# One two-bank PSUM tile against two one-bank tiles in the experts' first layer

## The chip, the cores and the metric

The kernel runs on one core of a Trainium2 chip. What is measured is the device time of one execution in microseconds (us). Five engines matter: PE (TensorE: matmuls, and PEld, its weight loads), ACT (ScalarE), DVE (VectorE), POOL (GpSimd) and SP (SyncE, which issues the DMA transfers). Each runs its own list of instructions in order and waits on semaphores for the others. PE writes its results to PSUM, which has 8 banks of 512 float32 per partition; ACT and DVE read them from there.

## The reference

Three parts follow each other: attention with a computed position bias, a mixture of 8 dense experts, and one more feed-forward layer with an ELU.

```
scores = q @ kT / sqrt(D) + bias(log1p|i-j| / log1p(i))     # B=2, H=8, S=576, D=64
x = softmax(scores) @ v                                     # -> (1152, 512)
P = exp(x @ w_gate - max); 8 rounds of row and column normalising
out = sum over 8 experts e of P[:, e] * (relu(x @ w1[e]) @ w2[e])    # w1: 512x1024, w2: 1024x512
g = elu(out @ w_in)                                         # 512 x 2048
return g @ w_out                                            # (1152, 512)
```

## The kernel before, in words

The experts and the last layer run as one chain of 20 half layers `he` (two for each of the 8 experts, four for the last feed-forward layer; each takes 512 of the hidden columns), and each half layer in two token groups `n` of 2 x 256 and 2 x 320 tokens (`NN`). All products are made of a high and a low part (three matmuls instead of one).

**First layer.** A pair (half layer, token group) is worked in two units `u`. A unit is a 2 x 2 block product by Winograd's form of Strassen's method: seven products of six matmuls each (`product`, line 526, the matmul on L537), written to three PSUM banks b1, b2 and b3. The table `PROD` says which product goes to which bank, and `l1` (line 684) issues them in the order 1, (4 of the unit before), 2, 5, 6, 3, 7. Products 1, 6, 7 and 4 follow each other in b1, products 5 and 3 in b2, product 2 is in b3. After each product something empties or uses the bank (`evac`, line 651):

- `fork` (L550) on ACT copies a bank to SBUF: p1 and u2, u3 from b1, p5 from b2.
- `add` (L569) on DVE adds a bank and an SBUF tile: c1 from b3 and p1, then c1's second half from b2 and u2, and c22.
- `hidden` (L600, L603, and for the last layer L628 to L647) applies the activation and splits the result into hh and hl.

**Second layer.** `l2` (line 706, the matmul on L724) multiplies hh and hl with the second weights into a PSUM tile y. `step` (line 997) mixes the matmuls of one pair's second layer between the first-layer products of the next, so that some 3 to 5 y matmuls stand between two products. They are missing in three stretches: in the first pair (there is no second layer yet), around the change from the experts to the last layer, and partly in the last layer's first pairs.

**Where the order comes from.** `Plan` records every operation with its costs and dependences; `order` (line 137) sorts them, PE's main matmuls in a fixed order and the rest greedily by estimated times; `emit` then writes the program in that sorted order. Semaphores are not set by the plan: the tile framework sets them while the program is written, from what each instruction reads and writes, tile by tile, in the order in which they are written.

**PSUM before.** Pool psA has two buffers of two banks each, psB two banks, psC0 and psD one each: 8 banks in all. The attention uses psA for the score products (`emit_qk`, L1215, read on DVE by L1225), psB for transposes and y, psC0 and psD for the rest. `unit` (line 674) takes one psA buffer for a unit: b1 is its first bank and b2 its second, both in one tile named `m`. b3 is the one buffer of psC0.

Of the kernel before, what the change touches and what calls it, by code (L numbers as in the profile page):

```python
# [86 lines left out]
class Plan:  # L87
# [3 lines left out]
    def buf(self, tag, bufs, alloc, tile=None):  # L91
        b = Buf(tag, alloc, tile)
        q = self.tags.setdefault(tag, [])
        b.prev = q[-bufs] if len(q) >= bufs else None
        b.before = q[-1] if q else None
        if b.prev is not None:
            b.prev.closed = True
        b.closed = False
        q.append(b)
        return b  # L100
# [120 lines left out]
def attention_moe_elu_ffn_kernel(  # L221
# [16 lines left out]
    def sb(name, bufs, st=ctx, side="left"):  # L238
        return st.enter_context(tc.tile_pool(name=name, bufs=bufs, side=side, reuse_waits="tile"))
# [6 lines left out]
    stp = sb("st", 1)  # L246
    dr = ctx.enter_context(tc.tile_pool(name="dr", bufs=1, space=bass.MemoryType.DRAM))

    def psum(name, bufs, shape):
        p = ctx.enter_context(tc.tile_pool(name=name, bufs=bufs, space=bass.MemoryType.PSUM))  # L250
        return lambda nm: p.tile(shape, F32, tag=name, name=nm)

    psA = psum("psA", 2, [128, 2, 512])
    psB = psum("psB", 2, [128, 512])
    psC = [psum("psC", 1, [128, 512]), psum("psD", 1, [128, 512])]

    csb = cp.tile([128, C_TOT], F32, name="csb")
    ident = csb[:, C_ID:C_ID + 128]
# [12 lines left out]
    def do_bg(n):  # L271
        for _ in range(min(n, len(bg))):
            bg.pop(0)()
# [106 lines left out]
    def build():  # L380
        op, buf = plan.op, plan.buf
# [291 lines left out]

        def unit(he, n, u):
            N = NN[n]
            a = buf("psA", 2, lambda: psA("m"))
            b3 = buf("psC0", 1, lambda: psC[0]("m3"))
            x = {"key": (he, n, u), "b1": (a, 0), "b2": (a, 1), "b3": (b3, 0)}
            x["ap"] = lambda k: b3.get()[:, 0:N] if k == "b3" else a.get()[:, int(k[1]) - 1, 0:N]
            return x  # L680

        prev = [None]
# [1 line left out]
        def l1(he, n):  # L684
            for u in range(2):
                x = None
                for i in (1, 4, 2, 5, 6, 3, 7):
                    if i == 4:
                        if prev[0] is None:
                            continue  # L690
                        product(prev[0], 4)
                        evac(prev[0], 4)
                    else:
                        if x is None:
                            x = unit(he, n, u)
                        product(x, i)
                        evac(x, i)
                    yield i
                prev[0] = x
# [395 lines left out]
    def first_fill():  # L1095
        do_bg(999)
        pools["ops1"] = sb("ops1", 1)
        pools["h0"] = sb("h0", 4)
        pools["fk"] = sb("fk", 1)
        build()  # L1100
        for x in emit_it:
            if x == "attn":
                return
            yield
# [456 lines left out]
    with tc.manual_schedule():  # L1561
        moe(attention(first_fill))
# [58 lines left out]
```

## Time and profile before

| | us |
|---|---|
| median of 3 runs (1196.85 to 1201.21) | 1200.32 |
| the profiled execution: time of the run | 1198.01 |
| the profiled execution: span from the first to the last instruction | 1196.2 |
| PE busy in it | 1159.5 |
| DVE busy | 909.6 |
| ACT busy | 630.7 |
| mean granted TensorE clock, share of full speed | 0.997 |

The profile names an instruction by its line, engine, operation and tiles (`m<-oh,w1h`: writes m from oh and w1h). A row of the timeline gives the start, the duration, and in square brackets the idle time of the engine ahead of it with the instruction that ended it. Matmuls overlap each other in the timeline: the next starts while the one before still runs out, so the pace is the distance of the starts, not the duration.

The experts begin at about 203 us of the span, the last feed-forward layer's first products at about 980 us.

### The profile page before, as it was taken

What the parts mean: (1) busy time and instruction counts of PE and PEld (TensorE: products, weight loads), DVE (VectorE), ACT (ScalarE), POOL (GpSimd) and SP (SyncE); (2) the same over time, 40 slices, a digit from 0 to 9 for tenths busy, and PEclk for the clock granted to TensorE, in tenths of its full rate; (3) what the DMA queues carried; (4) which work ended last, traced back from release to release, by engine and by line L of the source; (5) the groups of instructions that cost most, each with busy time, mean ns of one, the idle gap of its engine ahead of it and who ended that gap; (6) DMA issues with size and microseconds to landing.
All of it is one profiled execution on the core that took longest, in us unless ns stands there. A gap on an engine that the chain in (4) does not pass through costs nothing.

```text
span 1196.2 us, 19633 instructions
## 1 busy us (share of the span) xinstructions
PE 1159.5 (97%) x7432; PEld 994.0 (83%) x7432; DVE 909.6 (76%) x1936; ACT 630.7 (53%) x1428; POOL 67.8 (6%) x91
## 2 busy tenths in 40 slices
PE   7899999999999999999999999999999988999998
PEld 3467988888888888888888888888888876788887
DVE  7887888745687777878778788787765468788875
ACT  7997677644244343444443434444434346677763
POOL 0103452000000000000000000000000002000000
PEclk9999999999999999999999999999999999999999
DMA  7876641111012223232333242333311101111102
GB/s 211 243 230 199 195 120 38 39 58 51 31 53 80 79 89 104 91 106 89 88 106 89 79 121 74 106 89 106 88 54 51 47 19 36 36 53 36 36 1 79
DMA packets 36286, 104.78 MB, mean 88 GB/s; under 512 B 4065, under 2 KB 4193, under 8 KB 36193
## 3 DMA queue, kind: packets, MB, share of 16 engines
q1 hardware_dynamic: 36192, 103.54, 28.3%
q8 instruction: 58, 0.95, 0.3%
q14 instruction: 36, 0.29, 0.1%
HBM read 81.88 MB, written 21.64 MB: 87 GB/s over the span
## 4 chain that ended last, share of the span: by engine, by line
PE 91%; ACT 2%; DVE 2%; issue 1%; POOL 0%; DVEq 0%; ACTq 0%; POOLq 0%
PE y L724 41%; PE m L537 38%; PE sc L1215 3%; PE av L1297 3%; PE tr L1266 2%; PE bps L1419 1%; PE av L1307 1%; PE av L1294 1%; PE lg L880 0%; ACT et L1240 0%; DVE ol L437 0%; PE trl L1278 0%; PE x2t L974 0%; DVE c L569 0%; ACT o L1451 0%
## 5 line engine op out<-in xcount | busy, mean ns | idle before, releaser
L537 PE MATMUL m<-oh,w1h 128*128 128x256 f32 (+1 forms) x1120 | 335.6, 300 | 3.8 <-DVE c L569 1.4
L537 PE MATMUL m<-oh,w1l 128*128 128x256 f32 (+1 forms) x1120 | 330.2, 295 | 3.8 <-ACT u L550 1.6
L537 PE MATMUL m<-ol,w1h 128*128 128x256 f32 (+1 forms) x1120 | 330.1, 295 | 2.8 <-DVE c L569 1.3
L724 PE MATMUL y<-w2h,hh 128*128 128x512 f32 x720 | 285.1, 396 | 2.8 <-ACT hh L644 1.5
L724 PE MATMUL y<-w2l,hh 128*128 128x512 f32 x720 | 283.2, 393 | 0.8 <-DVE w2l L437 0.8
L724 PE MATMUL y<-w2h,hl 128*128 128x512 f32 x720 | 283.4, 394 | 0.0
L537 PEld LDWEIGHTS m<-oh,w1h 128*128 128x128 f32 x1120 | 210.5, 188 | 46.3 <-ACT u L550 13.4
L537 PEld LDWEIGHTS m<-ol,w1h 128*128 128x128 f32 x1120 | 210.8, 188 | 22.8 <-DVE c L569 1.9
L537 PEld LDWEIGHTS m<-oh,w1l 128*128 128x128 f32 x1120 | 210.7, 188 | 5.6 <-ACT u L550 2.3
L724 PEld LDWEIGHTS y<-w2h,hh 128*128 128x128 f32 x720 | 135.3, 188 | 18.7 <-ACT hh L644 2.2
L724 PEld LDWEIGHTS y<-w2h,hl 128*128 128x128 f32 x720 | 135.1, 188 | 18.0
L550 ACT ACTIVATE p<-m 128x256 f32<-128x256 f32 (+1 forms) x160 | 65.7, 411 | 159.3 <-PE m L537 155.2
L724 PEld LDWEIGHTS y<-w2l,hh 128*128 128x128 f32 x720 | 135.3, 188 | 16.3 <-DVE w2l L437 1.4
L550 ACT ACTIVATE u<-m 128x256 f32<-128x256 f32 (+1 forms) x160 | 65.8, 411 | 133.1 <-PE m L537 129.7
L600 ACT ACTIVATE hh<-c 128x512 fp32r<-128x512 f32 (+3 forms) x128 | 72.1, 563 | 110.1 <-DVE c L569 110.0
L755 DVE SCALAR_TENSOR_TENSOR acc<-y,P,acc 128x512 f32<-128x512 f32 x126 | 94.4, 749 | 38.8 <-PE y L724 36.5
L603 DVE SCALAR_TENSOR_TENSOR hl<-c,hh 128x512 fp32r<-128x512 f32 (+3 forms) x128 | 77.4, 605 | 20.6 <-ACT hh L600 18.8
L569 DVE TENSOR_TENSOR c<-m,u 128x256 f32<-128x256 f32 (+1 forms) x80 | 36.6, 458 | 72.7 <-PE m L537 71.1
L1225 DVE CUSTOM_DVE_ANT_0 et<-sc,bt 128x576 f32<-128x576 f32 (+1 forms) x80 | 57.9, 750 | 12.5 <-PE sc L1215 12.3
L1240 ACT ACTIVATE et<-et,nmx 128x576 f32<-128x576 f32 (+1 forms) x80 | 61.7, 775 | 0.3 <-DVE nmx L1225 0.3
L430 ACT ACTIVATE w2h<-raw 128x512 fp32r<-128x512 f32 x80 | 48.6, 625 | 21.8 <-PE y L724 12.4
L437 DVE TENSOR_TENSOR w2l<-raw,w2h 128x512 fp32r<-128x512 f32 x80 | 53.8, 690 | 2.4 <-ACT w2h L430 2.3
(138 smaller groups left out, 1547.1 us busy)
## 6 DMA issues: line engine op xcount, KB each, us to landing
raw<-w1p SPq DMA_DIRECT2D x32, 512.0 KB, 3.8
raw<-w2p SPq DMA_DIRECT2D x32, 512.0 KB, 3.5
scr<-o SPq DMA_DIRECT2D x36, 295.5 KB, 3.0
bt<-scr SPq DMA_DIRECT2D x16, 576.0 KB, 4.4
cw<-w1d SPq DMA_DIRECT2D x16, 512.0 KB, 4.4
wsc<-ca SPq DMA_DIRECT2D x32, 256.0 KB, 4.4
cw<-w2d SPq DMA_DIRECT2D x16, 512.0 KB, 4.3
raw<-wsc SPq DMA_DIRECT2D x16, 512.0 KB, 3.5
```

The source lines that it names most:

```text
L430: act.activation(out=dst(bh.get()), in_=src(), func=ACTF.Copy)
L437: lambda e: eng[e].tensor_tensor(out=dst(bl.get()), in0=src(), in1=dst(bh.get().bitcast(F32)), op=ALU.subtract),
L537: lambda e, w=w, o=o, j=j, k=k: pe.matmul(x["ap"](bank), w.get()[:, ai, j, :], o.get()[:, bi, j, :], start=(k == 0 and i in (1, 2, 5)), st ...
L550: lambda e: act.activation(out=b.get()[:, 0:N], in_=x["ap"](bank), func=ACTF.Copy),
L569: lambda e: eng[e].tensor_tensor(out=blk(b.get()[:, half * N:half * N + N], rev), in0=ap(p), in1=ap(q), op=ALU.add),
L600: op([("A", cA(w))], lambda e: act.activation(out=hh(), in_=ap(), func=ACTF.Relu), r=sk, w=wh, after=gate_)
L603: lambda e: dve.scalar_tensor_tensor(out=bl.get()[:, d], in0=ap(), scalar=0.0, in1=hhf(), op0=ALU.max, op1=ALU.subtract),
L724: lambda e, a=a, w=w, f=f, i=i, y=y, c=c: pe.matmul(y.get(), a.get()[:, c], w.get(), start=(f == 0 and i == 0), stop=(f == 3 and i == 2)),
L755: lambda e: dve.scalar_tensor_tensor(out=a.get(), in0=y.get(), scalar=P[0][:, n, e_:e_ + 1], in1=a.get(), op0=ALU.mult, op1=ALU.add),
L1215: pe.matmul(sc[h][0:r, x, 0:HALF], qs[:, h, qc], w[:, h, kc], start=not last, stop=last)
L1225: dve.tensor_tensor_reduce(out=e.rearrange("p (x j) -> p x j", x=2), in0=sc[0:r, :, 0:HALF], in1=biast[hp, t][0:r, h].rearrange("p (x j) - ...
L1240: act.activation(out=e, in_=e, func=ACTF.Exp, scale=-1.0, bias=nmx[0:r, h:h + 1], accum_out=sm[0:r, h:h + 1])
```

## The change

A unit takes two one-bank tiles, one from each of two new pools psM0 and psM1 with two buffers each, in place of one two-bank tile. Together they have the same four banks. As these pools have other shapes than psA, psA moves to the end of the PSUM pools, under a stack of its own, which is closed when the experts are set up, and the new pools are opened there. In the plan, b1 and b2 are now buffers of their own.

```
-    def psum(name, bufs, shape):
-        p = ctx.enter_context(tc.tile_pool(name=name, bufs=bufs, space=bass.MemoryType.PSUM))
+    def psum(name, bufs, shape, st=ctx):
+        p = st.enter_context(tc.tile_pool(name=name, bufs=bufs, space=bass.MemoryType.PSUM))
         return lambda nm: p.tile(shape, F32, tag=name, name=nm)
 
-    psA = psum("psA", 2, [128, 2, 512])
     psB = psum("psB", 2, [128, 512])
     psC = [psum("psC", 1, [128, 512]), psum("psD", 1, [128, 512])]
+    st_sc = ctx.enter_context(ExitStack())
+    psA = psum("psA", 2, [128, 2, 512], st_sc)
+    psM = []
...
         def unit(he, n, u):
             N = NN[n]
-            a = buf("psA", 2, lambda: psA("m"))
-            b3 = buf("psC0", 1, lambda: psC[0]("m3"))
-            x = {"key": (he, n, u), "b1": (a, 0), "b2": (a, 1), "b3": (b3, 0)}
-            x["ap"] = lambda k: b3.get()[:, 0:N] if k == "b3" else a.get()[:, int(k[1]) - 1, 0:N]
+            banks = [buf(f"psM{i}", 2, lambda i=i: psM[i]("m")) for i in range(2)]
+            banks.append(buf("psC0", 1, lambda: psC[0]("m3")))
+            x = {"key": (he, n, u)}
+            x.update((f"b{i + 1}", (b, 0)) for i, b in enumerate(banks))
+            x["ap"] = lambda k: x[k][0].get()[:, 0:N]
             return x
...
         pools["fk"] = sb("fk", 1)
+        st_sc.close()
+        psM.extend(psum(f"psM{i}", 2, [128, 512]) for i in range(2))
         build()
```

On every engine the instructions stand in the same order as before, with the same shapes; only line numbers, buffer numbers and the waits differ. The waits in square brackets name the semaphore of the engine that is waited for (Activation is ACT). Two places on PE show it.

PE in the experts' first pair, at products 5, 6 and the start of 3; m is the tile of the bank written, oh and ol are the tokens, w1h and w1l the weights, lg a matmul of the gate. Before:

```order
L537 MATMUL m_2977<-ol0_2696,w1h_2231 128x256
L537 MATMUL m_2977<-oh0_2695,w1l_2232 128x256
L537 MATMUL m_2977<-oh0_2695,w1h_2231 128x256
L537 MATMUL m_2977<-ol0_2696,w1h_2231 128x256
L537 MATMUL m_2977<-oh0_2695,w1l_2232 128x256
L537 MATMUL m_2977<-oh0_2695,w1h_2231 128x256 [waits Activation_49]
L537 MATMUL m_2977<-ol0_2696,w1h_2231 128x256
L537 MATMUL m_2977<-oh0_2695,w1l_2232 128x256
L880 MATMUL lg_3032<-oh0_2695,wg_hl_88 16x256 [waits DVE_49]
L537 MATMUL m_2977<-oh0_2695,w1h_2231 128x256
```

The same rows of the changed kernel:

```order
L539 MATMUL m_3016<-ol0_2696,w1h_2231 128x256
L539 MATMUL m_3016<-oh0_2695,w1l_2232 128x256
L539 MATMUL m_2984<-oh0_2695,w1h_2231 128x256 [waits Activation_49]
L539 MATMUL m_2984<-ol0_2696,w1h_2231 128x256
L539 MATMUL m_2984<-oh0_2695,w1l_2232 128x256
L539 MATMUL m_2984<-oh0_2695,w1h_2231 128x256
L539 MATMUL m_2984<-ol0_2696,w1h_2231 128x256
L539 MATMUL m_2984<-oh0_2695,w1l_2232 128x256
L883 MATMUL lg_3040<-oh0_2695,wg_hl_88 16x256 [waits DVE_49]
L539 MATMUL m_3016<-oh0_2695,w1h_2231 128x256 [waits Activation_49]
```

Before, products 5 (b2) and 6 (b1) write one tile, m_2977, and PE waits for ACT at the fourth matmul of product 6; the ACT instruction is the fork p5, which reads product 5's bank. Now they write two tiles, and PE waits at the first matmul of product 6, for the fork p1 (the last reader of b1), and at the first of product 3, for p5 (the last reader of b2).

PE in the middle of the experts, from the start of product 3 to the first matmul of product 7, with second-layer matmuls y between them. Before:

```order
L537 MATMUL m_10037<-oh1_2981,w1h_9713 128x320 [waits Activation_49]
L537 MATMUL m_10037<-ol1_3023,w1h_9713 128x320
L537 MATMUL m_10037<-oh1_2981,w1l_9722 128x320
L537 MATMUL m_10037<-oh1_2981,w1h_9713 128x320
L537 MATMUL m_10037<-ol1_3023,w1h_9713 128x320
L537 MATMUL m_10037<-oh1_2981,w1l_9722 128x320
L724 MATMUL y_10069<-w2h_10004,hl0_10025 128x512
L724 MATMUL y_10049<-w2h_10022,hh0_10056 128x512
L724 MATMUL y_10049<-w2l_10033,hh0_10056 128x512
L724 MATMUL y_10049<-w2h_10022,hl0_10062 128x512 [waits DVE_49]
L537 MATMUL m_10037<-oh1_2981,w1h_9713 128x320 [waits DVE_49]
```

The same rows of the changed kernel:

```order
L539 MATMUL m_10151<-oh1_2988,w1h_9775 128x320 [waits Activation_49]
L539 MATMUL m_10151<-ol1_3031,w1h_9775 128x320
L539 MATMUL m_10151<-oh1_2988,w1l_9784 128x320
L539 MATMUL m_10151<-oh1_2988,w1h_9775 128x320
L539 MATMUL m_10151<-ol1_3031,w1h_9775 128x320
L539 MATMUL m_10151<-oh1_2988,w1l_9784 128x320
L727 MATMUL y_10134<-w2h_10069,hl0_10090 128x512
L727 MATMUL y_10114<-w2h_10087,hh0_10121 128x512
L727 MATMUL y_10114<-w2l_10098,hh0_10121 128x512
L727 MATMUL y_10114<-w2h_10087,hl0_10127 128x512 [waits DVE_49]
L539 MATMUL m_10102<-oh1_2988,w1h_9775 128x320 [waits Activation_49]
```

Product 3 (b2) waited for the fork u2 of product 6 (b1), and now waits for p5 (b2), one ACT instruction earlier; product 7 (b1) waited for DVE's addition from b2, and now waits for u2 (b1).

## Rows read from the trace of the kernel before

**Rows 1.** The page's head: the span.

```profile
span 1196.2 us, 19633 instructions
```

**Rows 2.** Stretches: us, busy of PE, PEld, DVE, ACT, POOL, clock, DMA share, GB/s.

```profile
203.00:235.00 32.00, 28.64 (x192) 24.82 (x192) 24.40 (x55) 19.68 (x48) 1.76 (x3) 1.00 0.11 34
235.00:955.00 720.00, 719.00 (x4183) 634.63 (x4182) 533.51 (x1054) 298.93 (x640) 0.00 (x0) 1.00 0.26 80
```

**Rows 3.** PE's waits from 203 to 235 us: total us, times, longest.

```profile
PE m L537 <- DVE c L569: 1.2, 2, 0.7
PE m L537 <- ACT u L550: 1.0, 2, 0.5
PE m L537 <- ACT p L550: 0.9, 2, 0.5
```

**Rows 4.** PE's waits from 235 to 955 us.

```profile
PE m L537 <- DVE c L569: 0.7, 1, 0.7
```

**Rows 5.** PE's waits on L537's evacuations from 955 to 1035 us.

```profile
PE m L537 <- DVE c L569: 2.0, 4, 0.7
PE m L537 <- ACT u L550: 2.0, 4, 0.6
PE m L537 <- ACT p L550: 1.5, 3, 0.6
```

**Rows 6.** Timeline of PE at products 5 and 6 of the first pair.

```profile
206.83 0.28 PE L537 MATMUL m<-oh,w1l 128*128 128x256 f32 x1
...
207.18 0.28 PE L537 MATMUL m<-oh,w1l 128*128 128x256 f32 x1
207.94 0.39 PE L537 MATMUL m<-oh,w1h 128*128 128x256 f32 x1 [0.47 <-ACT p L550]
208.16 0.28 PE L537 MATMUL m<-ol,w1h 128*128 128x256 f32 x1
```

**Rows 7.** Timeline of ACT there.

```profile
207.50 0.38 ACT L550 ACTIVATE p<-m 128x256 f32<-128x256 f32 x1 [0.37 <-PE m L537]
```

**Rows 8.** Timeline of PE and ACT around product 3 in the middle of the experts.

```profile
901.02 0.44 ACT L550 ACTIVATE p<-m 128x320 f32<-128x320 f32 x1 [1.30 <-PE m L537]
...
902.80 0.40 PE L724 MATMUL y<-w2h,hh 128*128 128x512 f32 x1
902.83 0.44 ACT L550 ACTIVATE u<-m 128x320 f32<-128x320 f32 x1 [1.37 <-PE m L537]
903.04 0.39 PE L724 MATMUL y<-w2l,hh 128*128 128x512 f32 x1
...
903.32 0.42 PE L537 MATMUL m<-oh,w1h 128*128 128x320 f32 x1
903.58 0.31 PE L537 MATMUL m<-ol,w1h 128*128 128x320 f32 x1
...
903.73 0.31 PE L537 MATMUL m<-oh,w1l 128*128 128x320 f32 x1
```

**Rows 9.** Waits of PE's weight loads from 235 to 955 us.

```profile
PEld m L537 <- ACT u L550: 9.2, 28, 0.3
```

**Rows 10.** Waits of PE's weight loads from 1035 us on.

```profile
PEld m L537 <- ACT u L550: 1.9, 7, 0.3
```

**Rows 11.** The first layer's weight loads: ns min/median/max, first and last start.

```profile
L537 PEld LDWEIGHTS m<-oh,w1h x1120: 186/188/331, 203.5 to 1177.3; 128*128 128x128 f32 x187
```

**Rows 12.** Stretches at the change to the last layer, columns as in rows 2.

```profile
985.00:1000.00 15.00, 12.74 (x82) 11.04 (x83) 10.61 (x23) 9.29 (x23) 1.68 (x2) 1.00 0.18 60
1000.00:1014.00 14.00, 11.34 (x54) 8.25 (x53) 13.47 (x26) 9.75 (x21) 3.97 (x4) 1.00 0.00 1
```

**Rows 13.** Timeline of DVE, 985 to 1000 us: two waits for PE.

```profile
988.89 0.42 DVE L569 TENSOR_TENSOR c<-m,u 128x256 f32<-128x256 f32 x1 [1.83 <-PE m L537]
...
998.62 0.42 DVE L569 TENSOR_TENSOR c<-m,u 128x256 f32<-128x256 f32 x1 [1.09 <-PE m L537]
```

**Rows 14.** DVE's last score reads: ns min/median/max, first and last start.

```profile
L1225 DVE CUSTOM_DVE_ANT_0 et<-sc,bt x28: 742/751/758, 150.8 to 197.9; 128x576 f32<-128x576 f32 x20, 64x576 f32<-64x576 f32 x8
```

## The prediction

> **What bounds the kernel now.** I read the span [rows 1] first, then the busy times by stretch [rows 2], then PE's own waits in the same stretches [rows 3 to 5], and last the timeline around one wait of each kind [rows 6 to 8]. From 235 to 955 us PE is busy for 719.0 of 720 us at a granted clock of 1.00 and DVE for 533.5 [rows 2]: PE sets the time there, and only what holds PE up is worth anything. From 203 to 235 us PE is busy for 28.6 of 32 us [rows 2], so something else holds it a tenth of the time.
>
> What holds it up is in the lists of waits. In the stretches around the two changes of stage PE waits for the evacuations of its own first-layer products: for ACT's copies p and u and DVE's sum c, 6 times in the first [rows 3], once in the middle [rows 4] and 11 times in the second [rows 5]. That makes 18 waits of 9.3 us in all (3.1 + 0.7 + 5.5).
>
> The timeline shows what such a wait is. The last matmul of product 5 (bank b2) starts at 206.83; product 6 follows at once in the other bank, b1; the row at 207.18 is its third matmul, three starts later, so the pace is 0.12 us. Then PE stops until 207.94, and the releaser is ACT p [rows 6]. That copy reads product 5's bank b2, from 207.50 to 207.88 [rows 7]. PE was not to write b2 at all, but b1. So a matmul into one bank waits for a reader of the other bank, in the middle of a product, because both are one tile: the wait goes to whatever matmul is written into the program next after the copy. The copy is held as well: product 5 runs out at 206.83 + 0.28 = 207.11, but ACT starts only after the row at 207.18 has run out (207.46), since it waits for what was written into the tile before it.
>
> **The change, part by part.** No instruction is added, removed or moved on any engine; only waits differ. A matmul into b1 now waits for the last reader of b1, one into b2 for the last reader of b2.
>
> *The 18 long waits.* Price of one, from rows 6: the start at 207.94 comes 0.76 after that at 207.18 where the pace is 0.12, which is 0.64; the next comes 0.22 later instead of 0.12, another 0.10, since the weights could not be loaded ahead. That is 0.74 for 0.47 us of listed idle time, so a wait costs its idle time and 0.27. For all: 9.3 + 18 x 0.27 = 14.2 us. The next due wait is already over in most cases: product 3 waits for p5, which without the hold would start at 207.11 + 0.04, last 0.38 and release PE at about 207.6; product 6 ends, at 0.12 a matmul and with the gate's matmul behind it, at about 207.8.
>
> *The short waits in the middle.* At product 3 only three second-layer matmuls stand between it and product 6. The copy u of product 6's bank runs from 902.83 to 903.27; y matmuls stand 0.24 apart (902.80, 903.04), so product 3 could start at 903.27 and starts at 903.32; the next start comes 0.26 later where the one after it shows 0.15 [rows 8]. Together 0.16 us. Now product 3 waits for p5, done at 901.46 [rows 8], and the cost goes. The weight loads list 28 such waits [rows 9]: 28 x 0.16 = 4.5 us, all on PE's path, since PE is the bound there. In the last stretch there are 7 more [rows 10]; I take 0.10 for each, the weight load alone: 0.7 us.
>
> *What stays or comes.* Without second-layer matmuls in between, the margin of the next due wait is under 0.2 us (above), and the weight load ahead of it may still be late. Bounds for the 17 places in the two stage changes: nothing, or half of the old price wherever ACT is busy with something else (0.37 each, 6.3 us). I take the 0.10 of rows 6, the smallest stall that shows: 17 x 0.10 = 1.7 us.
>
> *DVE behind it.* From 1000 to 1014 us DVE is busy for 13.5 of 14 us [rows 12], and the second layer waits for it there. What PE wins ahead of that, DVE must win too. Between 985 and 1000 us PE is idle for 15 - 12.7 = 2.3 us [rows 12]; at 9.3 / 18 = 0.52 us each that is four or five of the waits, at 0.79 with the 0.27 about 3.4 us. DVE has 15 - 10.6 = 4.4 us of idle time in the stretch [rows 12], and the larger pieces of it are waits for PE's own late products (1.83 and 1.09 [rows 13]), which shrink with the gain. So between 0 and 3.4 us are lost; I take the middle, 1.7.
>
> *The pools.* Closing the score pool makes the first matmuls of the experts wait for the last read of a score tile. That read starts at 197.9 and lasts 0.75 [rows 14], so it is over at 198.7, and the first product starts at 203.5 [rows 11]. 4.8 us of cover: the cost is nothing. The attention's PSUM tiles change places, not number, and none of its waits differ.
>
> **The sum**: 14.2 + 4.5 + 0.7 - 1.7 - 1.7 = 16.0 us less. The profiled execution took 1198.0 us and would take 1182.0. The median of the runs is 1200.3, 2.3 above it; against that, the forecast is 1184.
>
> [...] The rows show PE stopped by the reader of a bank that it isn't writing [rows 6, 7, 8]. [...]
>
> A weight load lasts 188 ns [rows 11], and starts of undisturbed matmuls are 0.12 us apart [rows 6], so loads run beside the matmuls before them, and the 0.10 us after a stall is a load that could not. [...]
>
> **The rivals.**
> 1. *DVE and ACT become the bound in the stage changes.* For it: DVE's 13.5 of 14 us [rows 12]. Against it: its idle time just before, and 24.4 of 32 us in the first change [rows 2]. Price: the whole 3.4 instead of 1.7 and 6.3 instead of 1.7, another 6.3 us. Time 1200.3 - 9.7 = 1191. Chance 0.13.
> 2. [...] Time 1200. Chance 0.04.
> 3. *The tenth after each stall stays*, because weight loads are never hidden. Then 18 + 28 + 7 places give back 0.10 less, 5.3 us, and the 1.7 doesn't come on top: 19.4 - 5.3 - 1.7 = 12.4, time 1188. The pace against the 188 ns speaks against it. Chance 0.03.
> 4. *Slower: PE's writes and the reads of ACT and DVE get into each other's way* in PSUM, now that they overlap more. The first layer has 3 x 1120 matmuls [rows 11]. It takes 16.0 / 3360 = 4.8 ns on each to eat the gain, and 8 ns to end 10 us slower, at 1210. Against it: with ACT reading PSUM, matmuls start 0.24 apart at 902.80 and 903.04 [rows 8], and the next is late only by its wait. Chance 0.02.
>
> **How the numbers follow.** The forecast has 0.78. About 0.5% (6.0 us) is what a measurement of this kernel can tell from no change. The forecast and rivals 1 and 3 are faster by more than that, 0.94 in all; a part of rival 1 could end smaller, so 0.92. Rival 2 and that part make 0.06, rival 4 the 0.02. Range: at best nothing stays (19.4 us) and the runs fall as low as the lowest of before, 3.5 below the median: 1200.3 - 19.4 - 3.5 = 1177.4, so 1178. At worst rival 1, with the same spread above it: 1191 + 4 = 1195.
>
> **What would show it.** In the changed profile PE's waits for ACT p, ACT u and DVE c at the first layer's matmuls should be gone from 203 to 235 and from 955 to 1035 us but for single short ones, and so should ACT u in the list of weight-load waits. In the first pair ACT's p copy should start 0.3 us sooner after product 5. The waits of the second layer's y at about 1005 to 1014 us should stay. The span should fall by about 4 us before 235 us, by another 5 to 6 in the middle and by 6 around 1000 us. The prediction is wrong if the waits go and the span stays (rival 1), if they have other names (rival 2), or if the pace of the undisturbed matmuls rises (rival 4).

## The result and the profile after

The changed kernel takes 1179.9 us (median of 4 runs, 1177.6 to 1180.4), the kernel before, beside it, 1200.3 us. The ratio is 0.983, 95% interval 0.981 to 0.986: 20.4 us less, where 16.0 were forecast (1184, range 1178 to 1195). In a later set of runs, that of experiments 1 to 4, the same kernel gives 1180.05 against 1198.45, ratio 0.985 (0.983 to 0.986), 18.4 us less. The profiled execution of the changed kernel took 1180.22 us.

The page's head and its row of busy times, the changed kernel:

```profile
span 1178.4 us, 19626 instructions
...
PE 1150.9 (98%) x7432; PEld 1001.2 (85%) x7432; DVE 910.4 (77%) x1936; ACT 630.5 (54%) x1428; POOL 68.0 (6%) x91
```

The same stretches as in [rows 2] and the one around the change to the last layer; columns as there, in us: PE, PEld, DVE, ACT, POOL, granted clock, DMA share, GB/s. First the changed kernel:

```profile
203.00:235.00 32.00, 31.86 (x204) 29.32 (x203) 26.28 (x58) 20.45 (x49) 1.47 (x3) 0.89 0.11 34
235.00:955.00 720.00, 719.39 (x4220) 644.59 (x4219) 536.11 (x1059) 301.29 (x643) 0.00 (x0) 1.00 0.26 80
955.00:1035.00 80.00, 74.35 (x433) 64.66 (x432) 67.88 (x138) 57.10 (x124) 7.09 (x8) 0.98 0.12 36
```

and the last of them in the kernel before:

```profile
955.00:1035.00 80.00, 69.27 (x382) 57.60 (x381) 58.14 (x117) 46.91 (x102) 6.95 (x8) 0.98 0.06 20
```

PE's idle time goes from 3.4 to 0.1 us in the first stretch and from 10.7 to 5.7 in the last. In the middle PE was "busy" for 719.0 of 720 us already, so this view hides what was won there: a matmul that is late by a tenth still counts as busy (in [rows 8] the start 0.26 behind the one before it, where 0.15 follows, has no idle time listed). DVE's 67.9 us against 58.1 in the last stretch is no gain in speed: the changed kernel is some 9 us ahead by then, so the two windows hold different work. Between the same two matmuls (C and D below) DVE is busy for 60.9 us in the changed kernel and for 60.3 in the one before.

PE's waits say more. The list from 203 to 235 us, which had the six of [rows 3], is empty now. From 235 to 955 us the one of [rows 4] is gone and a single wait of y is left. From 955 to 1035 us (PE, what was waited for, total us, times, longest):

```profile
PE y L727 <- ACT hh L646: 1.5, 2, 1.1
PE y L727 <- DVE w2l L439: 0.8, 1, 0.8
PE m L539 <- DVE ol L439: 0.8, 1, 0.8
PE x2t L977 <- ACT xt L988: 0.7, 1, 0.7
PE y L727 <- ACT xt L988: 0.7, 1, 0.7
PE y L727 <- DVE acc L758: 0.7, 1, 0.7
PE m L539 <- ACT u L552: 0.5, 2, 0.4
```

Of the 11 waits of [rows 5], 5.5 us in all, two for ACT's u with 0.5 us are left. The other rows stood in the list of the kernel before too, with the same sizes; its largest were:

```profile
PE y L724 <- ACT hh L644: 1.5, 2, 1.1
PE y L724 <- DVE w2l L437: 0.8, 1, 0.8
PE m L537 <- DVE ol L437: 0.8, 1, 0.8
```

Among the weight loads' waits, ACT u has left the list of the middle (28 times in [rows 9]), and from 1035 us on one of 0.3 us stands where seven were [rows 10].

The place of [rows 8] in the changed kernel, timeline of PE around product 3, and then of ACT:

```profile
894.27 0.40 PE L727 MATMUL y<-w2h,hh 128*128 128x512 f32 x1
894.50 0.39 PE L727 MATMUL y<-w2l,hh 128*128 128x512 f32 x1
894.73 0.31 PE L539 MATMUL m<-oh,w1h 128*128 128x320 f32 x1
894.88 0.31 PE L539 MATMUL m<-ol,w1h 128*128 128x320 f32 x1
```

```profile
892.49 0.44 ACT L552 ACTIVATE p<-m 128x320 f32<-128x320 f32 x1 [1.41 <-PE m L539]
894.29 0.44 ACT L552 ACTIVATE u<-m 128x320 f32<-128x320 f32 x1 [1.36 <-PE m L539]
```

The copy u still runs up to the start of product 3, 894.73. But product 3 no longer depends on it: it starts 0.23 after the y matmul (0.28 before), the next one 0.15 later (0.26 before). The 0.16 us of the prediction is gone to the hundredth.

### Where the 20 us lie

The program's order is the same on PE in both kernels, so the same matmul can be looked up in each. I took five: A at the start of the experts (203.23 us in the kernel before), B at 240.03, C at 960.14, D at 1040.04, and the last one. Distances in us, each from the starts in one profiled execution; the experiments are those of the next section:

| | A to B | B to C | C to D | D to the last |
|---|---|---|---|---|
| kernel before | 36.80 | 720.11 | 79.90 (half clock) | 151.20 |
| pools alone changed | 36.75 | 718.83 | 78.39 | 151.21 |
| the change | 34.59 (half clock) | 713.66 | 71.73 (half clock) | 150.51 |
| the change again | 33.07 (half clock) | 713.66 | 70.17 | 150.52 |
| one-bank tiles in unit 0 | 34.78 (half clock) | 716.37 | 76.79 | 150.83 |
| one-bank tiles in unit 1 | 36.46 (half clock) | 716.69 | 71.78 | 150.84 |

"Half clock" marks stretches that hold a few microseconds at a granted clock of 0.50 (last section). Like against like, the change gives 8.2 us from C to D (79.90 - 71.73 with such a stretch in both, 78.39 - 70.17 with none), 0.7 at the end, and 5.2 in the middle (718.83 - 713.66; the 6.5 against the kernel before holds 1.3 that the pools alone show too, 720.11 - 718.83, at matmuls that waited for nothing). In the first stretch it gives 3.7 (36.75 - 33.07), although the second kernel's PE ran at the low clock (0.50) for some 3 us of it.

### The profile page after: what moved, and what is told of

Same layout as the page of the kernel before. It is cut to its first block, busy times and chain, and to the rows that moved or that the text cites. A ratio compares the mean times of both kernels' runs of the same rounds, so it can differ in the third digit from the quotient of the medians.

```text
span 1178.4 us, 19626 instructions
## 1 busy us (share of the span) xinstructions
PE 1150.9 (98%) x7432; PEld 1001.2 (85%) x7432; DVE 910.4 (77%) x1936; ACT 630.5 (54%) x1428; POOL 68.0 (6%) x91
## 4 chain that ended last, share of the span: by engine, by line
PE 90%; DVE 3%; ACT 1%; issue 1%; POOL 0%; DVEq 0%; ACTq 0%; POOLq 0%
PE y L727 41%; PE m L539 37%; PE sc L1220 3%; PE av L1302 3%; PE tr L1271 2%; PE bps L1424 1%; PE av L1312 1%; PE av L1299 1%; PE lg L883 0%; PE trl L1283 0%; DVE ol L439 0%; ACT et L1245 0%; PE x2t L977 0%; DVE w2l L439 0%; DVE et L1230 0%
## 5 line engine op out<-in xcount | busy, mean ns | idle before, releaser
L539 PE MATMUL m<-oh,w1h 128*128 128x256 f32 (+1 forms) x1120 | 331.3, 296 | 0.5 <-ACT u L552 0.5
L605 DVE SCALAR_TENSOR_TENSOR hl<-c,hh 128x512 fp32r<-128x512 f32 (+3 forms) x128 | 77.5, 606 | 20.3 <-ACT hh L602 18.4
L1230 DVE CUSTOM_DVE_ANT_0 et<-sc,bt 128x576 f32<-128x576 f32 (+1 forms) x80 | 58.0, 751 | 13.5 <-PE sc L1220 12.2
L439 DVE TENSOR_TENSOR w2l<-raw,w2h 128x512 fp32r<-128x512 f32 x80 | 53.9, 692 | 1.5 <-ACT w2h L432 1.5
```

Source lines behind the costliest of these rows:

```text
L439: lambda e: eng[e].tensor_tensor(out=dst(bl.get()), in0=src(), in1=dst(bh.get().bitcast(F32)), op=ALU.subtract),
L539: lambda e, w=w, o=o, j=j, k=k: pe.matmul(x["ap"](bank), w.get()[:, ai, j, :], o.get()[:, bi, j, :], start=(k == 0 and i in (1, 2, 5)), st ...
L605: lambda e: dve.scalar_tensor_tensor(out=bl.get()[:, d], in0=ap(), scalar=0.0, in1=hhf(), op0=ALU.max, op1=ALU.subtract),
L1230: dve.tensor_tensor_reduce(out=e.rearrange("p (x j) -> p x j", x=2), in0=sc[0:r, :, 0:HALF], in1=biast[hp, t][0:r, h].rearrange("p (x j) - ...
```

## The experiments

**1. The pools alone.** The score pool is moved to the end, closed at the experts, and a new pool is opened there, as in the change; a unit keeps its two-bank tile.

```
-            a = buf("psA", 2, lambda: psA("m"))
+            a = buf("psM", 2, lambda: psM[0]("m"))
...
+        st_sc.close()
+        psM.append(psum("psM", 2, [128, 2, 512]))
```

> The pools as in the change (score pool last, closed at the experts, a new pool opened there), but a unit keeps one two-bank tile. Theory (PE is held because two banks are one tile): nothing is won, 1200 us within 3 of the kernel before, ratio 0.998 to 1.002; PE's waits for ACT p, ACT u and DVE c from 203 to 235 us are 6 again, about 3 us in all, and 10 to 12 from 955 to 1035 us. Rival (the place of the banks, or the closing of the score pool, is what helps): about 1180 us.

Measured: 1198.46 us (12 runs) against 1198.45, ratio 1.0002 (0.9992 to 1.0012). PE's waits from 203 to 235 us are those of [rows 3] again:

```profile
PE m L539 <- DVE c L571: 1.2, 2, 0.7
PE m L539 <- ACT u L552: 1.0, 2, 0.5
PE m L539 <- ACT p L552: 0.9, 2, 0.5
```

From 955 to 1035 us there are 11 with 5.5 us. So neither the place of the banks nor the closing of the pool does anything that can be measured; the tiles do it.

**2 and 3. One unit of the pair at a time.** One-bank tiles only for the first unit of a pair, then only for the second. Each bank pool has one buffer there and the other unit a two-bank tile of its own; the order of the work is unchanged. For the first:

```
+            if u == 0:
+                banks = [buf(f"psM{i}", 1, lambda i=i: psM[i]("m")) for i in range(2)]
...
+            else:
+                a = buf("psN", 1, lambda: psM[2]("m"))
```

> One-bank tiles only in the first of a pair's two units (u = 0), the second keeps a two-bank tile; the waits that this loosens stood for about 8.3 us of stalls in the trace of the kernel before (203 to 235 us: 3.3; middle: 3.2; 955 to 1035: 1.5; tail 0.3). Theory (each stall of PE is a cost by itself, and the sum is theirs): 1192 us, 1189 to 1194. Rival (PE can win only if DVE and ACT win too, so that a stall taken away comes back in the next unit): under 4 us, 1197 or more. Rival (half is enough, since the slack of one unit covers the other): 1184 or less.

> The mirror of the last one: one-bank tiles only in the second unit (u = 1). Stalls on the waits that this loosens in the trace before: about 11.5 us (203 to 235 us: 1.4; middle: 2.7; 955 to 1035: 7.1; tail 0.3). Theory (stalls add up): 1189 us, 1186 to 1191, and the gains of the two halves add up to that of the change within 2 us. Rivals as there: 1197 or more, or 1182 or less.

Measured: 1191.45 us for the first unit, ratio 0.994 (0.993 to 0.996), and 1190.09 for the second, 0.993 (0.991 to 0.995); 7.0 and 8.4 us less. The first is as forecast, the second about a microsecond short of it (1189 was forecast, 1186 to 1191 as its range). Together they give 15.4 us where the whole change gives 18.4 in that set of runs, 3.0 apart where 2 at most was expected; the intervals of the three reach 1.7 to 2 us to either side, so that this can't be told from nothing by the times. The table of distances tells more. Against the pools alone, the halves add up to the whole wherever no half clock is in it: from C to D 1.6 + 6.6 against 8.2, at the end 0.4 + 0.4 against 0.7, in the middle 2.5 + 2.1 against 5.2. From A to B they don't (2.0 + 0.3 against 3.7): there each of the three executions pays for a half-clock stretch of its own. Taken matmul by matmul (the distance of each start from the one before it, against the pools alone), the matmuls that had waited and those right behind them give 3.4 + 1.7 against 5.1 from A to B, and all the others lose 1.4 in each of the three. Of the rivals, the one in which half the change gains nothing, and the one in which half is enough, both fall: stalls add up, one by one.

**4. The change once more**, beside the other three.

> The changed kernel once more, on the chip and beside the runs of the kernel before that the three others have. Both theories: 1180 us, 1177 to 1183. Of the stretch of half clock from 203.7 to 210.5 us: if it belongs to the change (PE falling to the low level because of its new rhythm), it is there again in this profile; if it is a matter of the single execution, it is gone or elsewhere, the mean clock is 0.995 or more, and the run takes about 3 us less, 1177.

Measured: 1180.05 us, ratio 0.985 (0.983 to 0.986). This execution shows what the half clock hid in the first profile, since the low level (0.50) ends within product 2. Timeline of PE, then of ACT:

```profile
209.16 0.41 PE L539 MATMUL m<-ol,w1h 128*128 128x256 f32 x1
209.38 0.36 PE L539 MATMUL m<-oh,w1l 128*128 128x256 f32 x1
209.57 0.28 PE L539 MATMUL m<-oh,w1h 128*128 128x256 f32 x1
...
210.16 0.28 PE L539 MATMUL m<-oh,w1l 128*128 128x256 f32 x1
210.28 0.28 PE L539 MATMUL m<-oh,w1h 128*128 128x256 f32 x1
...
210.63 0.28 PE L539 MATMUL m<-oh,w1h 128*128 128x256 f32 x1
...
210.99 0.28 PE L883 MATMUL lg<-oh,wg_hl 128*16 128x256 f32 x1
211.10 0.28 PE L539 MATMUL m<-oh,w1h 128*128 128x256 f32 x1
```

```profile
210.48 0.38 ACT L552 ACTIVATE p<-m 128x256 f32<-128x256 f32 x1 [1.45 <-PE m L539]
211.18 0.38 ACT L552 ACTIVATE u<-m 128x256 f32<-128x256 f32 x1 [0.32 <-PE m L539]
```

Product 5 runs from 209.57 to 210.16 + 0.28 = 210.44, and ACT's p starts at 210.48, 0.04 behind it; in [rows 6, 7] it was 0.39 behind. Product 6 runs from 210.28 through its fourth matmul at 210.63, where PE stopped before, to the gate's at 210.99, and product 3 follows at 211.10, with no start later than 0.12 after the last. p ends at 210.86, 0.24 ahead of product 3: the margin that the prediction put at about 0.2.

The half-clock stretch was there again, later and shorter (from 206 to 210 us), and the time was 1180, not 1177. So it isn't a matter of a single execution; that the change's rhythm causes it doesn't follow either (last section).

**5. The evacuation written first.** The kernel before with its two-bank tiles; PE's instructions are written 0.3 us later against those of the other engines.

```
-        self.out = sorted(out, key=lambda x: x[0])
+        self.out = sorted(out, key=lambda x: x[0] + (0.3 if x[1].pick == "T" else 0.0))
```

> The kernel before, two-bank tiles kept, but PE's instructions are written 0.3 us later against those of the other engines, so that an evacuation is written ahead of the next product's first matmul into the same tile. The evacuation then no longer waits for the next product's first three matmuls (it starts some 0.3 us sooner), and PE waits for it at the first matmul of the next product and not at its fourth. Theory (what costs is that PE stops for the other bank's reader, wherever in the product): at 0.64 + 0.10 us a long stall the time stays, 1196 to 1202 us, PE's waits from 203 to 235 us still 6 of some 3 us. Rival (what costs is that the evacuation starts late, so that its readers and PE behind them are late): 5 to 15 us faster, 1185 to 1193.

Measured: 1198.23 us against 1198.87, ratio 0.9992 (0.998 to 1.0005). Timeline of PE at the end of product 5 and the start of product 6, then ACT's copy of product 5:

```profile
207.16 0.28 PE L537 MATMUL m<-ol,w1h 128*128 128x256 f32 x1
207.28 0.28 PE L537 MATMUL m<-oh,w1l 128*128 128x256 f32 x1
208.03 0.38 PE L537 MATMUL m<-oh,w1h 128*128 128x256 f32 x1 [0.47 <-ACT p L550]
208.25 0.28 PE L537 MATMUL m<-ol,w1h 128*128 128x256 f32 x1
```

```profile
207.60 0.38 ACT L550 ACTIVATE p<-m 128x256 f32<-128x256 f32 x1
```

The copy now starts 0.04 after product 5 has run out (207.28 + 0.28 = 207.56), as in the changed kernel, and yet PE loses the same: 0.75 between the starts and 0.22 to the next, against 0.76 and 0.22 in [rows 6]. Only the place is another, the first matmul of product 6 instead of its fourth. The list of waits agrees (2.4 us in five from 203 to 235, 6.1 us in twelve from 955 to 1035). So what costs is that PE stops for a reader of the other bank. A sooner evacuation by itself is worth nothing that can be measured here.

**6. Low parts on POOL.** The changed kernel; what is left at the change to the last layer is tried. POOL may take the subtractions of L439.

```
-                [("D", cD(n))],
+                [("D", cD(n))] + ([("P", cP(n))] if alt else []),
```

> The changed kernel; POOL may take a subtraction that makes a low part (L439), where the plan finds DVE too late for it. It moves 8 of them around the change to the last layer. In the changed kernel PE still waits there 0.8 + 0.8 us for such subtractions and 1.5 us for ACT's hh. Theory (DVE is the bound at this change now, and only there): up to 3 us faster than the change, 1177 to 1180, and the waits for DVE's ol and w2l shrink. Rival (the chain through ACT is as long as DVE's, or POOL's slower instruction, 1.05 us against 0.41 us, is waited for): 1180 to 1184.

Measured: 1181.97 us, ratio to the kernel before 0.985 (0.983 to 0.988): no better than the change, as the rival had it, though for another reason. PE's longest waits from 955 to 1035 us:

```profile
PE y L727 <- DVE acc L758: 3.2, 1, 3.2
PE y L727 <- DVE hl L649: 1.0, 2, 0.7
```

and one of the moved subtractions on POOL:

```profile
998.02 1.09 POOL L439 TENSOR_TENSOR ol<-xt,oh 128x256 fp32r<-128x256 f32 x1 [0.73 <-ACT oh L432]
```

The waits for ol and w2l are gone from PE's list, as the theory said, but the plan has also put other work into another order, some of PE's matmuls included, and PE now waits 3.2 us for a y buffer that DVE frees (acc). So the run doesn't tell how much of the 5.7 us of idle time there is DVE's, nor whether a better order would win it.

**7. One buffer for b2**, so three banks in all instead of four.

```
-            banks = [buf(f"psM{i}", 2, lambda i=i: psM[i]("m")) for i in range(2)]
+            banks = [buf(f"psM{i}", 2 - i, lambda i=i: psM[i]("m")) for i in range(2)]
...
-        psM.extend(psum(f"psM{i}", 2, [128, 512]) for i in range(2))
+        psM.extend(psum(f"psM{i}", 2 - i, [128, 512]) for i in range(2))
```

> The changed kernel with one buffer for b2 instead of two, three banks for b1 and b2 in all. Theory (what helped is that the wait is for the own bank's reader, and the number of banks is not used up): b2 has only two products of seven, so that PE's next product in it comes after three others, and the time stays within 2 us of the change, 1178 to 1182 us. Rival (the two buffers together do the work, since a tile that is freed by one engine late blocks the next unit): half of the gain is lost, 1187 or more.

Measured: 1179.93 us, ratio 0.984 (0.982 to 0.986). Three banks with the right waits do what four do, and 18.9 us better than four with the wrong ones. PE's order is that of the change; on DVE and ACT the plan moved some instructions.

**8. The freed bank for y.** The kernel of 7, with the free bank as a third buffer of y.

```
+            k = ny[0] % 3
...
+            return buf("psB", 3, (lambda: psM[2]("y")) if k == 2 else (lambda: psB("y")))
```

> The last kernel (one buffer for b2), and the bank that it frees becomes a third buffer for the second layer's y. In the changed kernel PE waits for a y buffer (DVE's acc) for 0.3 us in the middle and 0.7 us at the change to the last layer. Theory (PE is busy for 719.4 of 720 us in the middle, so that no buffer there is worth anything): 1178 to 1181 us, at most 1 us below the change, which can't be told from it. Rival (at the change to the last layer the order of the work follows the third buffer, and PE finds work in the 5.6 us in which it idles there): 1175 to 1177.

Measured: 1179.73 us, ratio 0.984 (0.981 to 0.987). Not to be told from the change, as the theory said. None of the versions tried is faster than the change by more than its runs are apart.

## Why the prediction was right, and what was mis-sized

**The mechanism was right.** PE was held in the middle of a product by the reader of the other bank, because two banks were one tile. The runs show it from three sides: the same pools with a two-bank tile give nothing (1), each half of the tiles gives the stalls on its own waits (2, 3), and with two-bank tiles the stall stays when the evacuation starts as early as it can (5). The waits named ahead left the lists, the y waits stayed, and the p copy came 0.35 us sooner (0.3 was forecast).

**The terms.** By stretch, the prediction's three gains were 4.7 (six waits of 3.1 us and 6 x 0.27) before B, 5.5 in the middle (0.97 and 4.5), 8.5 between C and D (5.5 and 11 x 0.27) and 0.7 at the end: 19.4 us. The distances show 3.7 with a half-clock stretch inside, 5.2, 8.2 and 0.7. Matmul by matmul (experiment 4 against experiment 1) the places of the 18 long waits, each with the matmul behind it, give 13.5 us where 14.2 were forecast, and those of the short waits in the middle 4.3 for 27 of the 28, where 4.5 were. So the price of idle time plus 0.27 for a long wait, and 0.16 for a short one, held. The list of [rows 9] has another row in the kernel before, which the prediction passes over:

```profile
PEld m L537 <- DVE c L569: 5.9, 31, 0.9
```

One of the 31 is the long wait of [rows 4]; the other 30, with some 5 us of idle time, give 0.4 us together, where the 27 of [rows 9] give 4.3. So a row of this list doesn't tell what it costs; what counts is by how much the matmul behind the load comes late.

**The two deductions were mis-sized.** They took 3.4 us off the 19.4:

- *"the 0.10 of rows 6 ... 17 x 0.10 = 1.7 us"*, for next due waits that are over only just in time. It needs 17 late loads. The lists show none from 203 to 235 us and two short waits for u at the change to the last layer, 0.5 us of idle time, with 0.27 for each at most 1.0. In the place that experiment 4 shows, a margin of 0.24 us was enough.
- *"between 0 and 3.4 us are lost; I take the middle, 1.7"*, for DVE as the next bound. Here the lower bound was right: PE's waits for hh, w2l and ol at that change are of the same size in both kernels, and the 8.2 us from C to D leave 0.3 of the 8.5 for both deductions together. Yet DVE stays as full as it was. The full row of [rows 12] lies in one run of DVE instructions. Its first and its last, before and then after:

```profile
998.96 0.41 DVE L336 TENSOR_TENSOR st<-xt,xt 128x256 f32<-128x256 f32 x1
...
1017.31 0.48 DVE L569 TENSOR_TENSOR c<-m,p 128x320 f32<-128x320 f32 x1
```

```profile
984.38 0.43 DVE L338 TENSOR_TENSOR st<-xt,xt 128x256 f32<-128x256 f32 x1
...
1002.96 0.48 DVE L571 TENSOR_TENSOR c<-m,p 128x320 f32<-128x320 f32 x1
```

From start to start that is 18.35 us before (DVE busy for 17.8) and 18.58 after (18.3): nothing was won in it. But nothing of the forecast lay in it: of the 11 waits of [rows 5], eight are over by 999.1 us and three come from 1023 us on. Counted from C, the run begins 5.65 us sooner in the changed kernel, and DVE's idle time ahead of it is 5.6 us less, 3.8 of that in waits for PE's own first-layer products (6.7 before, 2.9 after). So what failed is the step from a full DVE to a loss of 1.7 us: the prediction had noted itself that this idle time shrinks with the gain [rows 13].

Without the deductions the forecast would have been 1181 (1200.3 - 19.4), a microsecond above the median; from the 1198.45 of the later set it would be 1179, a microsecond below its 1180.05. The half clock at the start of the experts, which takes 1.4 us back in experiment 4, was in no term. The lower end of the range was put at 1178 though its own sum gives 1177.4; the median lies above both.

**The rivals.** DVE and ACT as the bound (1191): no; DVE's full stretch is as long as before, and the stalls that went lay ahead of it and behind it. Rival 2, in which the waits go to other readers and last as long (1200): no; the next due readers were done (p ends 0.24 us ahead of product 3 in experiment 4). Nor was it enough that the products change banks: they do in the kernel before too, and in experiment 1, which gains nothing (1198.46 us against 1198.45). Weight loads never hidden (1188): no; in experiment 4 starts stay 0.12 us apart from 209.57 to 211.10, each of the first layer's matmuls with a weight load of its own, and such a load takes 0.19 us (188 ns [rows 11], and as the median in the changed kernel too). Slower by PSUM traffic (1210): no; in experiment 4 the pace stays at 0.12 while ACT's copy p reads from 210.48 to 210.86.

**The profiled execution** was forecast at 1182.0 and took 1180.2. By stage, "about 4 us before 235 us" came out smaller in the first profile (34.59 against 36.80 from A to B) because of the half clock, "5 to 6 in the middle" at 6.5 (5.2 against experiment 1), "6 around 1000" at 8.2.

## What to carry to other kernels

Look at a wait's releaser and ask which bank it reads. Where PE writes one bank and is released by the reader of another, the tile is too large: semaphores are set by tile here, so what is waited for separately should be a tile by itself; two buffers of a two-bank tile took 1198.87 us here and three separate banks 1179.93 (experiment 7). Price such stalls by the distances of the starts, also where the busy share says 99.9%: in the middle of this kernel nearly a quarter of the gain came from 28 delays of 0.16 us that only the weight loads' waits showed. And before taking something off a gain because another engine is nearly full, see whether the stalls lie inside its full stretch or ahead of it, where its idle time may itself be a wait for the stall that goes (3.8 of the 5.6 us here).

## What was not expected

All seven profiles of kernels with one-bank tiles show a few microseconds of half clock (0.50) at the start of the experts, with a mean of 0.76 to 0.88 from 200 to 214 us; none of the three with only two-bank tiles does (1.00). Views by stretch, columns as above, from 203 to 212 us: first the kernel before, then the change, then the change again.

```profile
203.00:212.00 9.00, 7.30 (x61) 6.05 (x61) 6.75 (x15) 4.79 (x12) 0.45 (x1) 1.00 0.01 2
```

```profile
203.00:212.00 9.00, 8.86 (x56) 8.06 (x55) 6.12 (x14) 4.13 (x10) 0.16 (x1) 0.62 0.01 2
```

```profile
203.00:212.00 9.00, 8.53 (x74) 7.39 (x73) 6.61 (x16) 5.32 (x16) 2.36 (x4) 0.81 0.00 0
```

In the change the clock falls within the microsecond from 203 to 204 (0.90 in it, 0.50 in the next), in which PE was busy for 0.86; in the kernel before PE was busy for 0.89 of the same one, and the clock stayed at 1.00. The first of PE's waits that differs comes at 207 us [rows 6], later than the fall. So the tiles can't have caused it there by the waits that they change, and why it is always these kernels stays open. The stretch isn't the only one: the kernel before has one from 1014 to 1018 us, the changed kernel from 999 to 1003, the repeat none near there, and all have one or more in the first 40 us. Over all runs the mean clock is the same (0.992 for the 17 runs of the kernel before beside experiments 1 to 4, 0.991 for the four of the change among them), so that no part of the gain is the clock's.
